# Windowed attention with global tokens and a Mish MLP on one core: the global product one unit later, a reserve on planned DMA landings, new planner constants

## The chip, the core and the metric

The kernel runs on one core of one Trainium2 chip. The metric is device time in microseconds of one execution; the time before is the median of three runs. The core has a matrix engine (PE), a vector engine (DVE), an activation engine (ACT), GpSimd (POOL), and SyncE (SP), which here issues every DMA.

## The reference

Attention with 8 batches and 8 heads of width 64: 512 local tokens see 32 global tokens and the local ones within 32 places; the 32 global tokens see all 544. The joined output, 4608 rows of 512, goes through an MLP of width 2048 whose activation is x tanh(softplus(x)) (Mish).

```python
    k_all = np.concatenate([k_g, k_l], axis=2)
    v_all = np.concatenate([v_g, v_l], axis=2)
    s_g = scale * np.matmul(q_g, k_all.transpose(0, 1, 3, 2))
    out_g = np.matmul(sm(s_g), v_all)
    s_ll = scale * np.matmul(q_l, k_l.transpose(0, 1, 3, 2))
    mask = np.abs(pos[:, None] - pos[None, :]) <= window
    s_ll = np.where(mask, s_ll, -1000000000.0)
    s_lg = scale * np.matmul(q_l, k_g.transpose(0, 1, 3, 2))
    a_l = sm(np.concatenate([s_lg, s_ll], axis=-1))
    out_l = np.matmul(a_l, np.concatenate([v_g, v_l], axis=2))
...
    h = x @ w_in
    sp = np.where(h > 20.0, h, np.log1p(np.exp(np.minimum(h, 20.0))))
    g = h * np.tanh(sp)
    return (g @ w_out).astype(np.float32)
```

The weights arrive as 64-bit floats, the rest as 32-bit. The kernel gets its accuracy on PE from pairs of f16 numbers (a high part and the rest), so that each product of the MLP and each P V takes three f16 matmuls.

## The kernel before, in words

**Attention.** The work is cut into units (batch b, head pair hp, quarter t of the 512 queries), 16 a batch and 128 in all. A unit has scores (L649 where q and k are used in f32, for the first eight pairs; L656 from f16 pairs afterwards), a masked row maximum on DVE (L662, into P), exp on ACT (L671), the split of P into high and low f16 (ph: L326 or L328, and L723), its transpose (batch 0 on PE, L695 and L700; later by a DMA transpose from ph to pt, L482), and P V (U, L740). After the fourth quarter x = U / sum is formed (L750), split (L759) and transposed into xh and xl, the input of the MLP. The global queries are done once per head pair: scores g (L780) and maximum (L794) at t = 2, exp (L802), the split of P on DVE (L814), one DMA transpose into gpt (L482), and their P V, g_pv (gu, L829: 15 matmuls), whose result ACT or DVE puts into xg. xg is the input of the MLP's last block.

**MLP.** 17 blocks of 256 rows, each in 8 steps. A step multiplies by one slice of w_in (h, L872, 24 matmuls of 256 columns), takes Mish on ACT (e, L915), splits the result into G (L328, L928 on DVE) and multiplies by one slice of w_out (o, L940, 12 matmuls of 512 columns). Twelve steps' G fit into its ring.

**Weights.** 32 pieces of 512 KB are loaded; three DVE instructions each turn 64-bit numbers into f32 (L405, L407, L414); PE sums squares (ws, L427) for a scale; then 16 splits into high and low f16 (high on ACT or DVE; low on DVE, L459). The first eight L459 are w_in's slices, the last eight w_out's. Step i of a block needs split i for h and split 8 + i for o.

**What sets the order.** The function slot(u) records the tasks of one slot in turn: the scores of unit u + 1, P V of unit u - 1, and the MLP steps that M1S puts there (h in its slot, G one later, o two later). Each task has a priority by its place in the record, the weights' tasks by a slot number of their own (CONV for conversions, FIRST for splits). Then Plan.order goes through the tasks once: it keeps a time for each engine, for the DMA queue and for every result, always takes the task that could start first (by priority where several could), and writes the tasks out in that order. So the order on every engine is fixed when the program is built. A DMA's result counts as there at its end in the queue plus DMA_OUT = 400 ns. A weight load may be issued only while the planned DMA backlog is under BULK.

Of the kernel before, what the change touches and what calls it, by code (L numbers as in the profile page):

```python
# [51 lines left out]
class Plan:  # L52
# [6 lines left out]
    DMA_IN, DMA_OUT, DMA_DEPTH = 1500, 400, 5500  # L59
    TICK, COLUMNS = 10240 / 3, 3060  # L60
    LOYAL = 800
    TABLE = 1283

    def __init__(self):
# [74 lines left out]
    def order(self):  # L139
# [9 lines left out]
        start, done, on = [None] * N, [0] * N, [None] * N  # L149
        columns = {}  # L150
        served = 0

        def tensor(t, ns, rows):

            while ns > 1e-6:
                k = int(t / self.TICK + 1e-9)
                slow = 1 if columns.get(k - 1, 0) >= self.COLUMNS else 2
                d = min(ns * slow, (k + 1) * self.TICK - t)
                columns[k] = columns.get(k, 0) + d / slow * 2.4 * rows
                ns -= d / slow  # L160
                t += d
            return t

        def enter(n):
            engs, fn, deps, after, new, pri, rows, table = self.tasks[n]
            for e, ns in engs:
                t = max([done[d] + self.HOP[on[d]][e] for d in deps] + [start[a] for a in after] + [0])
                bisect.insort(queue[e], (pri, n, ns, t))

        def first(e):  # L170

            best = None
            for pri, n, ns, t in queue[e]:
                t = max(t, free[e]) + (self.TABLE if e == ACT and self.tasks[n][7] not in (None, self.table) else 0)
                if e == DMA and len(ns) > 2:
                    t = max(t, served - ns[2])
                e0 = self.tasks[n][0][0][0]
                if e0 != e and free[e0] <= t + self.LOYAL:
                    continue
# [9 lines left out]
        for _ in range(N):  # L189
            t, pri, e, n, ns = min(c for c in map(first, free) if c)  # L190
            start[n], on[n] = t, e
            if e == ACT:
                self.table = self.tasks[n][7] or self.table
            for x, _ in self.tasks[n][0]:
                queue[x] = [c for c in queue[x] if c[1] != n]
            if e == PE:
                ns = tensor(t, ns, self.tasks[n][6]) - t
            if e == DMA:
                issue, ns = ns[:2]
                free[e] = t + issue + max(0, served - t - self.DMA_DEPTH)  # L200
                served = max(served, t + self.DMA_IN) + ns
                done[n] = served + self.DMA_OUT
            else:
                free[e] = done[n] = t + ns
            for u in users[n]:
                left[u] -= 1
                if not left[u]:
                    enter(u)
# [15 lines left out]
def attn_mish_kernel(ctx: ExitStack, tc: tile.TileContext, qt, kt, qt0, kt0, mxs, vm, vg, qg, w1, w2, consts_in, out, w64):  # L224
# [77 lines left out]
    def dma(kib):  # L302
        return 410, kib * 3.05

    def bulk(kib):
        return dma(kib) + (BULK,)

# [658 lines left out]
        UNITS[:16] = sorted(UNITS[:16], key=lambda x: (x[2] // 2, x[1], x[2]))  # L966
    steps = [(blk, i) for blk in range(NBLK) for i in range(NF)]

    LEAD0 = 13.709
    PACE = 0.958  # L970
    TAIL = 14
    M1S = []
    for s in range(len(steps)):
        at = int(LEAD0 + PACE * s) if s < 2 * NF else s + TAIL
        if s % NF == 0 and steps[s][0] < 2 * B:
# [8 lines left out]
    def att(fn, b, *a):  # L984
        pl.late = LATE_B * (b == 1)
        fn(b, *a)
        pl.late = 0

    def slot(u):
# [3 lines left out]
        fu, bu, vu = unit(u + 1), unit(u), unit(u - 1)  # L993
        b, hp, t = (u // 16, u % 16 // 4, u % 4) if bu else (0, 0, -1)
# [22 lines left out]
        if more2 and t == 3:  # L1017
            pl.late = LATE_K * (b == 0)
            k_hi(*n2)
            k_lo(*n2, 0)  # L1020
        if more1 and t == 0:
            pl.late = LATE_K * (b == 0)
            k_lo(*n1, 1)
        if more1 and t == 1:
            pl.late = LATE_K * (b == 0)
            q_hi(*n1)
# [34 lines left out]
            blk_out(m2[0])  # L1061
        if m2:
            m2_mm(*m2, 0)
        if t == 3:
            att(g_pv, b, hp)
        if m2:
            m2_mm(*m2, 1)
        if more2 and t == 1:
            pl.late = LATE_L * (b == 0)
            k_load(*n2)  # L1070
        if more2 and t == 3:
            pl.late = LATE_L * (b == 0)
            q_load(*n2)
# [11 lines left out]
        if bu and b == 0 and hp == 3 and t == 3:  # L1085
            pl.late = LATE_V
            b_load(b + 1)
# [24 lines left out]
                g_split(b + 1)  # L1112


    BULK = 2744.748
    LAG = 8
    ORDER = "k0 q0 m b k1 q1 w0 w1 g w2 w3 k2 q2 w4 w5 w6 w7 k3 q3 w8 w9 w10 w11 w12 w13 w14 w15"
    CONV1 = 10
    RATE1 = 0.05
    CONV2 = 15.31  # L1120
    RATE2 = 1.5
    FIRST1 = 9.206
    STEP1 = 1.5
    FIRST2 = 4.746
    STEP2 = 2.5
    AHEAD_DMA = 2.301
    LATE_K = 39.044
    LATE_L = 289.135
    LATE_B = 0
    LATE_V = 0  # L1130

    def weights():
        for k in range(32):
            at = CONV1 + RATE1 * k if k < 16 else CONV2 + RATE2 * (k - 16)
            if k >= 16:
                pl.slot = at - AHEAD_DMA
                w_load(k)
# [10 lines left out]
            if k == 19:  # L1148
                for j in range(8):
                    pl.slot = FIRST1 + STEP1 * j  # L1150
                    w_split(j)
        for j in range(8):
            pl.slot = FIRST2 + STEP2 * j
            w_split(8 + j)
# [4 lines left out]
    for x in ORDER.split():  # L1159
        a, n = x[0], int(x[1:] or 0)  # L1160
# [92 lines left out]
```

## Time and profile before

| | |
|---|---|
| three runs | 1061.85, 965.97, 967.1 us |
| median | 967.1 us |
| profiled execution, its own time | 966.51 us |
| its span, first to last instruction | 964.7 us |
| mean granted PE clock | 0.977 |
| PE busy, first 100 us / 100 to 200 / 200 to 800 / 800 to 900 / last 65 | 76.9 / 96.7 / 586.6 / 100.0 / 54.4 us |
| DVE busy, first 100 us / 100 to 200 / 200 to 300 | 83.6 / 87.8 / 91.7 us |
| half-clock stretches of PE in the records | 49.8 to 63.5, 70.3 to 84.0, 94.2 to 101.0, 138.6 to 142.0, and from 957.8 us |

A row of the groups gives the line, engine, operation and tiles, the shape, the count, the busy time and the mean of one in ns, then the idle time ahead of such instructions and what ended it. A row of the waits gives who waited for whom, the total in us, how often, and the longest. A row of a stage gives its borders and length, the busy time and count of PE, PE's weight loads, DVE, ACT and POOL, the granted PE clock, the share of the DMA engines and GB/s. A row in order of time gives the start, the length, the instruction, and in brackets the idle time ahead of it. Matmuls that follow each other overlap in these rows, so the time from one start to the next is what a matmul costs.

### The profile page before, as it was taken

What the parts mean: (1) busy time and instruction counts of PE and PEld (TensorE: products, weight loads), DVE (VectorE), ACT (ScalarE), POOL (GpSimd) and SP (SyncE); (2) the same over time, 40 slices, a digit from 0 to 9 for tenths busy, and PEclk for the clock granted to TensorE, in tenths of its full rate; (3) what the DMA queues carried; (4) which work ended last, traced back from release to release, by engine and by line L of the source; (5) the groups of instructions that cost most, each with busy time, mean ns of one, the idle gap of its engine ahead of it and who ended that gap; (6) DMA issues with size and microseconds to landing.
All of it is one profiled execution on the core that took longest, in us unless ns stands there. A gap on an engine that the chain in (4) does not pass through costs nothing.

```text
span 964.7 us, 20600 instructions
## 1 busy us (share of the span) xinstructions
PE 914.6 (95%) x7988; PEld 630.5 (65%) x7988; DVE 680.7 (71%) x1789; ACT 623.4 (65%) x1270; POOL 15.8 (2%) x28
## 2 busy tenths in 40 slices
PE   6787989999999999999999999999999999999995
PEld 3554774667676767667666676666666677666663
DVE  6799989788997889767777677768777755222221
ACT  4657667587876778776777777778877787211110
POOL 2000000000000000000000000000000000000000
PEclk9967999999999999999999999999999999999998
DMA  8897539988998669765576675665756342100000
GB/s 271 259 290 219 150 109 204 206 180 235 245 275 211 153 151 201 145 149 120 142 161 147 128 169 136 139 143 122 184 129 144 75 102 51 34 1 22 1 22 22
DMA packets 214010, 141.00 MB, mean 146 GB/s; under 512 B 176664, under 2 KB 188184, under 8 KB 212888
## 3 DMA queue, kind: packets, MB, share of 16 engines
q1 hardware_dynamic: 213912, 139.69, 60.2%
q8 instruction: 62, 1.02, 0.5%
q14 instruction: 36, 0.29, 0.1%
HBM read 75.15 MB, written 8.91 MB: 87 GB/s over the span
## 4 chain that ended last, share of the span: by engine, by line
PE 52%; DVE 23%; DMA 13%; ACT 4%; issue 4%; SPq 1%; DVEq 0%; ACTq 0%
PE o L940 23%; PE h L872 19%; DMA gpt<-gph 5%; DMA pt<-ph 3%; DMA vraw<-in_vm 3%; PE U L740 3%; DVE P L662 2%; PE s L656 2%; DMA kn_m<-in_mxs 2%; DVE kl L594 2%; PE s L649 2%; DVE G L928 2%; PE gu L829 2%; DVE gmx L794 1%; DVE W L407 1%
## 5 line engine op out<-in xcount | busy, mean ns | idle before, releaser
L940 PE MATMUL o<-W,G 128*128 128x512 f16 x1632 | 388.7, 379 | 0.2 <-ACT ob L326 0.2
L872 PE MATMUL h<-xh,W 128*128 128x256 f16 x2048 | 377.6, 274 | 2.3 <-ACT e L915 2.3
L872 PEld LDWEIGHTS <-W 128*128 128x128 f16 x3264 | 312.0, 98 | 66.6 <-issue 9.3
L872 PE MATMUL h<-xl,W 128*128 128x256 f16 x1024 | 280.2, 274 | 0.0
L940 PEld LDWEIGHTS <-G 128*128 128x128 f16 x1632 | 157.4, 98 | 148.0 <-issue 3.5
L915 ACT ACTIVATE e<-h,c 128x512 f32<-128x512 f32 (+1 forms) x137 | 92.7, 684 | 140.3 <-PE h L872 139.3
L671 ACT ACTIVATE P<-P,nm 128x192 f32<-128x192 f32 (+1 forms) x256 | 117.7, 460 | 52.2 <-DVE nm L662 49.9
L328 DVE TENSOR_SCALAR G<-e,c 128x512 f16<-128x512 f32 (+1 forms) x126 | 60.4, 480 | 128.7 <-ACT e L915 128.6
L662 DVE CUSTOM_DVE_ANT_0 P<-s,consts 128x192 f32<-128x192 f32 (+1 forms) x256 | 90.5, 366 | 44.1 <-PE s L656 38.3
L928 DVE SCALAR_TENSOR_TENSOR G<-e,c,G 128x512 f16<-128x512 f32 (+1 forms) x137 | 101.9, 744 | 3.0
L723 DVE SCALAR_TENSOR_TENSOR ph<-P,ph 128x384 f16<-128x384 f32 (+1 forms) x112 | 65.1, 584 | 40.0 <-ACT ph L326 39.3
L915 ACT ACT_TABLE_LOAD x62 | 79.5, 1283 | 1.1
L740 PEld LDWEIGHTS <-pt 96*128 96x128 f16 (+1 forms) x1536 | 62.7, 99 | 17.3 <-DMA pt<-ph 7.4
L671 ACT ACT_TABLE_LOAD x54 | 69.3, 1283 | 1.0
L326 ACT ACTIVATE ph<-P 128x384 f16<-128x384 f32 (+1 forms) x107 | 57.9, 545 | 11.3 <-DMA pt<-ph 9.0
L740 PE MATMUL U<-va,pt 128*128 128x64 f16 (+1 forms) x768 | 57.4, 195 | 4.9 <-DMA pt<-ph 3.9
L740 PE MATMUL U<-vc,pt 96*128 96x64 f16 x768 | 56.4, 195 | 0.0
L671 ACT ACTIVATION_READ_ACCUMULATOR P<-P,nm 128x1 f32 x256 | 47.9, 187 | 0.0
L656 PEld LDWEIGHTS <-qs 128*128 128x128 f16 x384 | 34.7, 98 | 17.9 <-issue 0.2
L649 PE MATMUL s<-kn,qn 64*128 64x192 f32 (+1 forms) x128 | 36.8, 483 | 7.3 <-DMA qn<-in_qt 4.5
L656 PE MATMUL s<-ks,qs 128*128 128x192 f16 (+1 forms) x192 | 42.2, 253 | 0.0
L656 PE MATMUL s<-kl,qs 128*128 128x192 f16 (+1 forms) x192 | 42.2, 252 | 0.0
(121 smaller groups left out, 914.2 us busy)
## 6 DMA issues: line engine op xcount, KB each, us to landing
kraw<-in_kt SPq DMA_DIRECT2D x24, 640.0 KB, 4.8
kn_m<-in_mxs SPq DMA_DIRECT2D x24, 544.0 KB, 4.9
qraw<-in_qt SPq DMA_DIRECT2D x24, 512.0 KB, 3.9
out<-ob SPq DMA_DIRECT2D x34, 256.0 KB, 2.5
vraw<-in_vm SPq DMA_DIRECT2D x8, 1024.0 KB, 6.2
wraw<-in_w SPq DMA_DIRECT2D x16, 512.0 KB, 5.3
W<-in_w SPq DMA_DIRECT2D x16, 512.0 KB, 6.2
vc<-vf SPq DMA_DIRECT2D x32, 128.0 KB, 2.4
```

What stands on the lines that cost most here:

```text
L326: A.activation(out=dst, in_=src, func=AF.Copy, scale=c)
L328: V.tensor_scalar(dst, src, c, None, ALU.mult)
L649: pl.add(PE, mm(1, 4 * w), lambda: T.matmul(X[s][:, :w], X[q][r, part, t * 128:(t + 1) * 128], X[k][r, part, c0:c0 + w], start=True, stop= ...
L656: T.matmul(X[s][:, :w], X[qs][:, h, t * 128:(t + 1) * 128], X[k][:, h, c0:c0 + w], start=(i == 0), stop=(i == 1))
L662: pl.add(DVE, 69 + 1.04 * w, lambda: V.tensor_tensor_reduce(out=X[P][:, h, :w], in0=X[s][:, :w], in1=mask[:, m0:m0 + w], scale=-SCALE, sca ...
L671: pl.add(ACT, 94 + 0.832 * w + 186, lambda: A.activation(out=X[P][:, h, :w], in_=X[P][:, h, :w], func=AF.Exp, bias=X[nm], scale=-1.0, accu ...
L723: pl.add(DVE, dve(n), lambda: V.scalar_tensor_tensor(p_part(X[ph], t, 1), p_src(X[P], t), PSC, p_part(X[ph], t, 0), ALU.mult, ALU.subtract ...
L740: T.matmul(X[u][:, t, h, :], X[pt][:k, p * 4 + h * 2 + c, :], X[vx][:k, t, vl, h * 64:(h + 1) * 64], start=(n == 0), stop=(n == 5))
L872: T.matmul(X[h][:, f * TB:(f + 1) * TB], wh(i, wl)[:, off:off + 128], X[x][:, d, o:o + TB], start=(n == 0), stop=(n == 11))
L915: chain(blk, i, ACT, 587, lambda a, z: A.activation(out=X[e][:, a:z], in_=hv(blk, i)[:, a:z], func=AF.Mish, bias=0.0, scale=X[c][:, 0:1]), ...
L928: chain(blk, i, DVE, 663, lambda a, z: V.scalar_tensor_tensor(gp(1, blk, i)[:, a:z], X[e][:, a:z], X["c", blk][:, 2:3], gp(0, blk, i)[:, a ...
L940: T.matmul(X[o], gp(g, blk, i)[:, f, t * 128:(t + 1) * 128], wh(8 + i, wl)[:, f * 512:(f + 1) * 512], start=(i == 0 and n == 0), stop=(i = ...
```

## The change

Three things change. First, g_pv of a head pair was recorded in the slot of its last quarter (t == 3); it is now recorded in the slot behind that (when the unit whose P V is taken is the last quarter). Second, the planner adds SPARE = 900 ns to a DMA's landing where the planned time is over 180 us; nothing in the program waits for it, it only puts the users of the data later in the order. Third, sixteen planner constants have new values.

```diff
+    SPARE = 900
...
-                done[n] = served + self.DMA_OUT
+                done[n] = served + self.DMA_OUT + (self.SPARE if t > 180000 else 0)
...
-    LEAD0 = 13.709
-    PACE = 0.958
-    TAIL = 14
+    LEAD0 = 20.957
+    PACE = 0.709
+    TAIL = 15
...
-        if t == 3:
-            att(g_pv, b, hp)
+        if vu and vu[2] == 3:
+            att(g_pv, *vu[:2])
...
-    BULK = 2744.748
+    BULK = 4939.749
...
-    CONV2 = 15.31
-    RATE2 = 1.5
+    CONV2 = 2.779
+    RATE2 = 1.422
```

With LEAD0, PACE and TAIL the rule for M1S gave each MLP step the slot of its number plus 17; it now gives its number plus 20. CONV1, RATE1, FIRST1, STEP1, FIRST2, STEP2, AHEAD_DMA, LATE_K, LATE_L and LATE_V are the rest of the constants. Line numbers of the changed kernel are one higher from the place where SPARE stands.

The order changes on every engine. Two places of it follow. The first is ACT in batch 4, head pair 1, from the second half of the global queries' exp (gP) to the scaling of their product (xg from gu, which PE computes just ahead). P and ph are the next pair's local units, e is Mish. Before:

```order
L802 ACTIVATE gP_1_6394,gs_1_6395<-g_1_1_6312,gmx_1_6330 64x256
L671 ACTIVATE P_74,sums_2_6398<-P_74,nm_2_0_1_6428 128x192
L326 ACTIVATE ph_80<-P_74 128x4x96
L915 ACT_TABLE_LOAD
L915 ACTIVATE e_6465<-h_6377,c_4539 128x512
L319 CAST xs_1_6486<-x_1_6482 128x512
L326 ACTIVATE xg<-gu_1_6496,sv_5322 64x32 x2
```

and now, from the row behind that gP on:

```order
L672 ACTIVATE P_74,sums_2_6252<-P_74,nm_2_0_0_6248 128x192
L916 ACT_TABLE_LOAD
L916 ACTIVATE e_2_6288<-h_2_6147,c_4789 128x512
L916 ACTIVATE e_3_6304<-h_3_6231,c_4789 128x512
L672 ACT_TABLE_LOAD
L672 ACTIVATE P_74,sums_2_6252<-P_74,nm_2_0_1_6290 128x192
L327 ACTIVATE ph_80<-P_74 128x4x96
L672 ACTIVATE P_75,sums_2_6252<-P_75,nm_2_1_0_6347 128x224
L672 ACTIVATE P_75,sums_2_6252<-P_75,nm_2_1_1_6366 128x224
L327 ACTIVATE ph_81<-P_75 128x2x224
L320 CAST xs_1_6381<-x_1_6370 128x512
L327 ACTIVATE xg<-gu_1_6399,sv_5181 64x32 x2
```

One more Mish and a whole unit of the next pair (P_75, ph_81) now stand between the global exp and the product, and Mish there belongs to a step three or four numbers lower.

The second place is DVE at the last two splits of w_out (the fifteenth and sixteenth L459; kn_m are the maxima of a later batch, vf and x belong to batch 1). Before:

```order
L814 SCALAR_TENSOR_TENSOR gph_88<-gP_1_1968,gs_1_1969,gph_88 64x544
L459 SCALAR_TENSOR_TENSOR W<-W,sw 128x1024
L723 SCALAR_TENSOR_TENSOR ph_80<-P_74,ph_80 128x4x96
L585 SCALAR_TENSOR_TENSOR qs_1_1937<-qraw_1_1824,sk_1723,qs_1_1937 64x1024
L459 SCALAR_TENSOR_TENSOR W<-W,sw 128x1024
L750 TENSOR_TENSOR x_1_2090<-U_1_1920,rs_1_1963 128x512
```

and now, from the row behind the fifteenth split on:

```order
L724 SCALAR_TENSOR_TENSOR ph_80<-P_74,ph_80 128x4x96
L528 TENSOR_REDUCE mx_3_2105<-kn_m_0_1895 128x1
L751 TENSOR_TENSOR x_1_2127<-U_1_1924,rs_1_1918 128x512
L663 ISA P_76,nm_2_2_0_2137<-s_2_2_0_2109,consts 128x224
L663 ISA nm_2_2_0_2137 128x1
L610 SCALAR_TENSOR_TENSOR vf_3_2129<-vraw_803,sv_1537,vf_3_2129 128x4x128
L760 TENSOR_TENSOR xs_1_2139<-x_1_2127,xs_1_2139 128x512
L663 ISA P_76,nm_2_2_1_2155<-s_2_2_1_2124,consts 128x224
L663 ISA nm_2_2_1_2155 128x1
L663 ISA P_74,nm_2_3_0_2158<-s_2_3_0_2142,consts 128x192
L663 ISA nm_2_3_0_2158 128x1
L460 SCALAR_TENSOR_TENSOR W<-W,sw 128x1024
```

Rows of batch 1's attention that stood behind the last split (x, its split xs, three row maxima, a v split) now stand ahead of it.

More of the change, by code (lines that the diff above doesn't have):

```diff
@@ L1112, in slot @@
                 g_split(b + 1)
-    BULK = 2744.748
+    BULK = 4939.749
     LAG = 8
     ORDER = "k0 q0 m b k1 q1 w0 w1 g w2 w3 k2 q2 w4 w5 w6 w7 k3 q3 w8 w9 w10 w11 w12 w13 w14 w15"
-    CONV1 = 10
-    RATE1 = 0.05
-    CONV2 = 15.31
-    RATE2 = 1.5
[L1122 to L1128, printed above, removed]
+    CONV1 = -2
+    RATE1 = 1.119
+    CONV2 = 2.779
+    RATE2 = 1.422
+    FIRST1 = 8.288
+    STEP1 = 1.452
+    FIRST2 = 16.719
+    STEP2 = 0.743
+    AHEAD_DMA = 4.88
+    LATE_K = 220.655
+    LATE_L = 1.986
     LATE_B = 0
-    LATE_V = 0
+    LATE_V = 106.565
     def weights():
```

## The prediction

> **What bounds the kernel now.** I read the page's first block, then the table of stages, then the waits by stage, then the order of time at the places where a wait ends.
>
> ```profile
> span 964.7 us, 20600 instructions
> PE 914.6 (95%) x7988; PEld 630.5 (65%) x7988; DVE 680.7 (71%) x1789; ACT 623.4 (65%) x1270; POOL 15.8 (2%) x28
> ```
>
> PE is busy for 95% of the span. The other 50 us, and the time at a lower clock, are what a new order can win or lose: the change adds and removes no matmul. The table of stages says where they lie (span of the stage, busy time by engine, then the granted clock):
>
> ```profile
> 0.00:20.00 20.00, 14.53 (x44) 8.29 (x44) 11.10 (x46) 10.49 (x30) 6.79 (x13) 1.00 0.82 283
> 20.00:168.00 148.00, 127.15 (x1055) 86.29 (x1054) 135.30 (x338) 96.83 (x210) 1.46 (x4) 0.87 0.73 206
> 168.00:226.00 58.00, 57.91 (x521) 38.10 (x520) 47.62 (x137) 41.31 (x99) 0.35 (x1) 1.00 0.87 188
> ```
>
> From 20 to 168 us DVE is busy for 135.3 of 148 us and PE for 127.2, at a mean clock of 0.87: here DVE, which converts the weights, sets the pace. What ends that stage is the last split of w_out, the sixteenth row of L459. In order of time, DVE's ninth and sixteenth splits and the first out-projection matmuls, then the batch-1 step of the same kind where G is what PE needs:
>
> ```profile
> 138.81 1.28 DVE L459 SCALAR_TENSOR_TENSOR W<-W,sw 128x1024 f16<-128x1024 f32 x1
> 141.84 1.55 PE L940 MATMUL o<-W,G 128*128 128x512 f16 x6
> 166.63 1.28 DVE L459 SCALAR_TENSOR_TENSOR W<-W,sw 128x1024 f16<-128x1024 f32 x1
> 167.28 4.05 PE L940 MATMUL o<-W,G 128*128 128x512 f16 x18
> 224.38 0.74 DVE L928 SCALAR_TENSOR_TENSOR G<-e,c,G 128x512 f16<-128x512 f32 x1
> 225.24 1.46 PE L940 MATMUL o<-W,G 128*128 128x512 f16 x6
> ```
>
> The ninth split ends at 140.1 and o starts at 141.8. The sixteenth ends at 167.9; the row of 18 begins with six matmuls of the step before, so the last step of block 0 starts at about 168.6. At 225 us a G ends at 225.1 and its matmul starts at 225.2. PE follows DVE to there without a gap, then DVE falls out of the path. After 168 us PE is short of work only in single waits, which the waits of PE in 180 to 850 us list (total, times, longest):
>
> ```profile
> PE gu L829 <- DMA gpt<-gph: 8.6, 9, 1.6
> PE U L740 <- DMA pt<-ph: 3.3, 5, 1.4
> PE g L780 <- DVE nm L662: 0.6, 1, 0.6
> PE o L940 <- ACT ob L326: 0.2, 1, 0.2
> ```
>
> So 12.7 us in the middle, of which 8.6 are the global queries' product waiting for its transposed probabilities. The end is the same rows in both orders and counts for nothing.
>
> **The waits in the middle.** The prices of PE work come from the chain of waits at full clock:
>
> ```profile
> 183.23 1.29 PE o L940 x6
> 184.52 0.35 PE U L740 x12
> 184.88 1.31 PE h L872 x12
> 189.15 0.44 PE gu L829 x15
> 189.59 0.63 PE s L649 x4
> ```
>
> (The last row is two score matmuls: each f32 one has two records.) In PE's order I count what stands between the last score matmul of the global queries (second g) and their product gu. For batch 4, pair 1 it was 48 h, 30 o, 24 U and 4 s, which is 5.2 + 6.5 + 0.7 + 0.3 = 12.7 us; now it is 60 h, 30 o, 24 U and 8 s, 14.5 us. Counted so over batches 3 to 7 the distance was 8 to 15 us, and is now 14 to 16, nearly everywhere the same 14.6. The largest wait was 1.6 us, so 2 to 5 us more work in between covers it. I take 8.0 of the 8.6, and as bounds 0 (something behind it is late instead) and 8.6; a loss is excluded as long as the distance grew. Of what moves with the 15 matmuls, the two scalings to xg are read only by the last block; vf and va are held a slot longer, and behind them on SP stand the seven moves of the pair after next, which in the new SP order have one transpose of P more ahead of them.
>
> The reserve of 0.9 us, together with the MLP's slots (each step three slots later than before, 20 instead of 17 after its number), puts the local products later behind their scores: the least distance from a pair's second score matmul to U, counted the same way over batches 3 to 7, goes from 9.0 to 10.8 us. Of the 3.3 us of U waits, five of at most 1.4 us, I take 2.0 away; bounds 0 and 3.3. What is late next there would be G for o: the least distance from h to its o was 4.6 us and is 8.2 in the blocks 2 and 3, and 6 to 10 in both after that, so I expect no new wait.
>
> **The DVE-bound stage.** The other constants (conversions, splits, loads, BULK, batch 1's v) only reorder what DVE, PE and SP do to 225 us, and are costed together. I count the rows of DVE ahead of the sixteenth split, before and now. The kinds are the same but for: 5 more L662, 2 more L594, one more each of L527, L609, L750, L759, of the copy to ks, and of an xg scaling (none ran on DVE before; ACT's took 0.27), and one G copy less. Prices from the groups of instructions with shapes kept apart (the last row in order of time):
>
> ```profile
> L662 DVE CUSTOM_DVE_ANT_0 P<-s,consts 128x224 f32<-128x224 f32 x128 | 46.8, 384 | 14.8 <-PE s L656 12.0 <-PE s L649 2.4
> L594 DVE SCALAR_TENSOR_TENSOR kl<-kraw,sk,ks 128x640 f16<-128x640 f32 x48 | 41.6, 866 | 0.0
> L527 DVE TENSOR_REDUCE mx<-kn_m 128x1 f32<-128x1088 f32 x24 | 30.6, 1277 | 3.5 <-DMA kn_m<-in_mxs 3.5
> L609 DVE SCALAR_TENSOR_TENSOR vf<-vraw,sv,vf 128x512 f16<-128x512 f32 x32 | 23.7, 746 | 3.5 <-ACT vf L326 3.3
> L750 DVE TENSOR_TENSOR x<-U,rs 128x512 f32<-128x512 f32 x32 | 21.9, 684 | 8.6 <-PE U L740 8.5
> L759 DVE TENSOR_TENSOR xs<-x,xs 128x512 f16<-128x512 f32 x28 | 19.2, 687 | 5.0 <-ACT xs L319 4.9
> L328 DVE TENSOR_SCALAR ks<-kraw,sk 128x1280 f16<-128x1280 f32 x14 | 12.3, 878 | 0.5 <-DMA kraw<-in_kt 0.3
> L328 DVE TENSOR_SCALAR G<-e,c 128x512 f16<-128x512 f32 x124 | 59.7, 482 | 125.9 <-ACT e L915 125.8
> 33.84 0.27 ACT L326 ACTIVATE xg<-gu,sv 64x32 f32<-64x32 f32 x1
> ```
>
> 1.9 + 1.7 + 1.3 + 0.7 + 0.7 + 0.7 + 0.9 + 0.3 less 0.5 is 7.7 us. Neighbouring rows overlap: all DVE durations of the trace add up to 780 us where the page has 680.7 busy, 0.87 of them, so the split comes 6.7 us later. Against that, PE has more of its work behind it by then. Ahead of the last step of block 0 stand 12 h, 12 U, 15 gu, 7 f32 s and 3 f32 g more: 1.3 + 0.35 + 0.45 + 2.2 + about 1.0 (g at the price of three s) is 5.3 us that needn't be done later. The end moves by 6.7 - 5.3 = +1.4 us. Bounds: +6.7 if PE gains nothing by its advance, and -9 if three quarters of DVE's 12.7 us of idle time between 20 and 168 us went. I see no reason for the latter: the largest gap of that idle is x waiting for PE's first U,
>
> ```profile
> 32.87 0.69 DVE L750 TENSOR_TENSOR x<-U,rs 128x512 f32<-128x512 f32 x1 [3.51 <-PE U L740]
> ```
>
> and in the new order the statistics of eight weight pieces instead of four (32 ws matmuls, not 16, each behind a DVE conversion) stand ahead of that U on PE, so DVE gets there later but finds it late again. At the 225 us point the new order has five more us of PE work ahead and under three more of DVE: no bound any more. Nor should a load be late, though DVE now reaches the first pieces of w_out 3 to 12 us sooner. DVE's waits on weight loads between 20 and 168 us were
>
> ```profile
> DVE W L405 <- DMA W<-in_w: 0.8, 2, 0.6
> ```
>
> and of the bytes that stand ahead of each piece in SP's new order, as many had been moved in this trace at least 1.9 us before DVE would reach the piece.
>
> The new order has one hole: between the eleventh and the twelfth split stand 25 DVE rows (7 before) of about 11 us, while PE has 7 us of work between the steps that need them. Released by the tenth split, PE would stand ready about 2 us before the twelfth. The trace shows what such a wait draws:
>
> ```profile
> 137.64 0.27 PE L872 MATMUL h<-xh,W 128*128 128x256 f16 x1 [2.19 <-ACT e L915]
> 135.20:138.60 3.40, 1.21 (x12) 0.95 (x10) 2.23 (x11) 3.36 (x6) 0.37 (x1) 1.00 0.64 141
> 138.60:142.00 3.40, 3.40 (x18) 2.44 (x17) 3.16 (x12) 2.47 (x4) 0.00 (x0) 0.50 0.37 80
> ```
>
> A wait of 2.19 us, then 3.4 us at a granted clock of 0.50: 1.7 us of matmul time lost. The splits that follow hide about half of it, so I add 0.9 us (bounds 0 and two such windows, 3.4).
> The Trainium skill (TensorE: Matmul & The Clock Gate, HAM oscillation) asks only that PE have no idle gaps over about 3.4 us. By that rule the 2 us wait would cost no clock and this term would be nothing, 957.9 in all; the trace does not agree, since 2.19 us were enough at 135 us.
>
> **What changes nothing.** LATE_K and LATE_L are used only in batch 0, for pairs whose scores take the unsplit path, so no instruction is placed by them. TAIL has no effect, since each step is put at least one slot behind the step ahead of it.
>
> **The sum.** The profiled execution took 966.5 us (span 964.7), 0.6 under the median of 967.1. 966.5 - 8.0 (gu) - 2.0 (U) + 1.4 (DVE stage) + 0.9 (clock) = 958.8 us.
>
> **Rivals.**
> *No gain (chance 0.14).* The waits are filled, but another wait takes their place: PE's order is static, and DVE and ACT follow PE in the middle, so G for o or the next score's bank (three for s, g and gu) can be late in turn. For: one gu wait stood where the distance was already 14 us. Against: DVE and ACT have a quarter of their time free there. 966.5 + 1.4 + 0.9 is about 968 us.
> *Slower (0.13).* The hole before the twelfth split and the steps behind it make PE wait at each split, and each wait draws a half-clock window; PE at half clock then loses its 5.3 us of advance. Place: 140 to 180 us. Price: 6.7 + 4 windows of 1.7 = 13.5; 966.5 - 10.0 + 13.5 = 970 us. It decides if the waits at the splits come to over 2 us each, at four of them.
> *A faster start (0.13).* The conversions that now stand earlier fill DVE's idle time. For: 12.7 us are there to fill. Against: DVE's own count went up by 6.7, and the first U is as late. With 9.5 of it gone, 958.8 - 9.5 is about 949 us.
>
> **Chances and range.** The forecast has 0.60. The range of 950 to 968 takes in the forecast, the case without gain and the slower half of the faster start; the slower case and the other half (0.20) are left out. Two per cent of the median, about what a measurement of this kernel can tell from no change, is 19.3 us: 947.8 and 986.4. Half of the faster start lies below (0.07), the far end of the slower case above (0.03), the rest (0.90) between.
>
> **What would show it.** Right: PE's gu wait under 1 us in 180 to 850 us, U under 2; the sixteenth L459 ending at 173 to 177 us, with o right behind it; a PE gap of about 2 us near 155 us with a half-clock window behind it; PE's last matmul 7 to 8 us earlier. Wrong: a gu wait still above 4 us (the distance was not the cause); the sixteenth split before 168 us (DVE's idle time went); several windows at half clock between 140 and 180 us; or new PE waits on G or nm in the middle that add up to 8 us.

## The result and the profile after

| | before | after |
|---|---|---|
| median | 967.1 us (six runs, 963.86 to 1061.85) | 958.58 us (six runs, 957.19 to 960.59) |
| ratio | | 0.9917, 95% interval 0.9896 to 0.9938 |
| profiled execution, its own time and span | 966.51, 964.7 us | 957.52, 955.7 us |
| PE's last matmul ends | 954.4 us | 945.8 us |

One execution of before (1061.85 us) and one of e6 below (2360.64 us) took far longer than the rest, and the ratios leave them out. The forecast was 958.8 us and a change within 2%; both came. Whether the reasons came too is the question of the rest. The first block of the page, after:

```profile
span 955.7 us, 20644 instructions
PE 908.4 (95%) x7988; PEld 628.1 (66%) x7988; DVE 668.0 (70%) x1774; ACT 630.5 (66%) x1283; POOL 19.6 (2%) x28
```

The matmuls are as many as before. The stages of the prediction, and the middle in two pieces (columns as before: borders, length, busy time and count of PE, PEld, DVE, ACT, POOL, granted PE clock, DMA share, GB/s), of after:

```profile
20.00:168.00 148.00, 122.56 (x1046) 84.69 (x1046) 135.58 (x348) 97.48 (x216) 2.92 (x4) 0.92 0.71 201
168.00:226.00 58.00, 55.71 (x496) 34.91 (x495) 44.40 (x130) 41.98 (x106) 0.78 (x1) 1.00 0.79 176
180.00:300.00 120.00, 114.84 (x1103) 79.11 (x1101) 101.68 (x285) 94.79 (x201) 3.93 (x4) 1.00 0.89 208
300.00:850.00 550.00, 548.82 (x5066) 386.74 (x5063) 384.93 (x1031) 402.64 (x790) 5.91 (x7) 1.00 0.63 138
```

and the last two of before:

```profile
180.00:300.00 120.00, 118.47 (x1115) 82.62 (x1116) 106.99 (x277) 92.63 (x187) 3.40 (x5) 1.00 0.96 225
300.00:850.00 550.00, 538.06 (x4992) 378.00 (x4990) 391.77 (x1055) 397.78 (x793) 4.12 (x6) 1.00 0.60 133
```

From 300 to 850 us PE is busy for 548.8 of 550 us where it was busy for 538.1: there the change wins over 10 us. From 180 to 300 us it is busy for 3.6 us less than before: there it loses some back. The waits of PE in 180 to 850 us, after:

```profile
PE U L741 <- DMA pt<-ph: 3.7, 8, 0.7
PE gu L830 <- DMA gpt<-gph: 1.7, 2, 1.0
PE h L873 <- ACT e L916: 0.7, 1, 0.7
```

gu fell from 8.6 to 1.7 us, U did not fall. The start, in DVE's and PE's order of time (the w_out splits from the twelfth split on; PE's steps that need them, and its two waits for o; then x, which waited for PE's first U):

```profile
154.03 1.27 DVE L460 SCALAR_TENSOR_TENSOR W<-W,sw 128x1024 f16<-128x1024 f32 x1
...
172.47 1.28 DVE L460 SCALAR_TENSOR_TENSOR W<-W,sw 128x1024 f16<-128x1024 f32 x1
```

```profile
136.70 0.38 PE L941 MATMUL o<-W,G 128*128 128x512 f16 x1 [0.69 <-ACT W L327]
138.02 0.81 PE L941 MATMUL o<-W,G 128*128 128x512 f16 x3 [0.94 <-DVE W L460]
...
156.22 1.47 PE L941 MATMUL o<-W,G 128*128 128x512 f16 x6
...
175.59 1.69 PE L941 MATMUL o<-W,G 128*128 128x512 f16 x7
```

```profile
38.85 0.69 DVE L751 TENSOR_TENSOR x<-U,rs 128x512 f32<-128x512 f32 x1 [4.09 <-PE U L741]
```

The sixteenth split ends at 173.75 us (forecast 173 to 177; before 167.9), and the last step of block 0 starts at 175.6 (before 168.6).

**A ledger of PE's time.** To compare orders that do the same work in another sequence, I take for a matmul its start less the priced PE work ahead of it (prices as in the prediction: h 0.109, o 0.216 us, and so on; 887.3 us in all). It grows where PE waits or runs at half clock. One price is too high (g's), so it sinks by 7 to 8 us from 300 to 850 us in a kernel that never waits; differences between kernels hold. From one matmul's start to the next, less the price, it also says what each wait really cost.

| us | before | after | difference | of it gu | U | all else |
|---|---|---|---|---|---|---|
| at the last step of block 0 | 57.0 | 58.5 | +1.5 | | | |
| growth from there to 300 us | +2.2 | +6.0 | +3.8 | +2.0 | +1.9 | -0.1 |
| growth from 300 to 850 us | +7.7 | -6.0 | -13.7 | -11.6 | -1.7 | -0.4 |

The sum is -8.4 us; PE's last matmul came 8.6 us sooner.

### The profile page after: what moved, and what is told of

Read it like the earlier page. It is cut to its first block, busy times and chain, and to the rows that moved or that the text cites. A ratio compares the mean times of both kernels' runs of the same rounds, so it can differ in the third digit from the quotient of the medians.

```text
span 955.7 us, 20644 instructions
## 1 busy us (share of the span) xinstructions
PE 908.4 (95%) x7988; PEld 628.1 (66%) x7988; DVE 668.0 (70%) x1774; ACT 630.5 (66%) x1283; POOL 19.6 (2%) x28
## 4 chain that ended last, share of the span: by engine, by line
PE 67%; DVE 18%; DMA 8%; ACT 3%; issue 2%; SPq 1%; POOL 0%; DVEq 0%; ACTq 0%
PE o L941 29%; PE h L873 27%; PE U L741 3%; DMA pt<-ph 3%; PE s L657 3%; DMA kn_m<-in_mxs 2%; PE g L781 2%; DVE W L415 2%; DVE W L408 2%; DVE P L663 2%; DMA vraw<-in_vm 1%; PE s L650 1%; DVE W L460 1%; DMA gpt<-gph 1%; DVE mx L528 1%
## 5 line engine op out<-in xcount | busy, mean ns | idle before, releaser
L327 ACT ACTIVATE ph<-P 128x384 f16<-128x384 f32 (+1 forms) x112 | 61.0, 546 | 14.5 <-DMA pt<-ph 12.3
L803 ACT ACTIVATE gP<-g,gmx 64x288 f32<-64x288 f32 x64 | 30.3, 474 | 21.7 <-DVE gmx L798 21.6
```

The source lines that it names most:

```text
L327: A.activation(out=dst, in_=src, func=AF.Copy, scale=c)
L803: pl.add(ACT, 464, lambda part=part, c0=c0, c1=c1: A.activation(out=X[P][:, c0:c1], in_=X["g", b, hp, part][:64, 0:c1 - c0], func=AF.Exp, ...
```

## The experiments

Two theories stood at the outset. *Distance* (the prediction's): gu waited because too little PE work stood between the global scores and their product; g_pv one unit later is what ends it. *Plan*: the waits come from where the planner put loads, transposes and engines' work around g_pv, and the reserve (or the new constants) is what ends them, with or without the distance. All ratios are to the kernel before on the chip of that run, where its median was 966.3 to 967.1 us.

| kernel | median us | ratio, interval | start (last step of block 0) | growth to 300 | waits of gu, U, others from 300 to 850, start to start |
|---|---|---|---|---|---|
| before | 967.1 | 1 | 57.0 | 2.2 | 11.6, 3.0, 0.6 |
| after | 958.58 | 0.9917 [0.9896, 0.9938] | 58.5 | 6.0 | 0, 1.3, 0.7 |
| e1 after, g_pv back | 960.72 | 0.9941 [0.9918, 0.9963] | 58.5 | 6.8 | 3.4, 0, 0.2 |
| e2 after, no reserve | 973.21 | 1.0070 [1.0047, 1.0093] | 59.8 | 18.2 | 0, 2.6, 4.5 |
| e3 before, g_pv later | 965.67 | 0.9986 [0.9968, 1.0004] | 56.0 | 3.8 | 0, 6.7, 4.2 |
| e4 before, reserve | 959.33 | 0.9928 [0.9907, 0.9949] | 56.4 | 1.6 | 1.9, 5.5, 1.9 |
| f1 before, reserve on gpt | 961.93 | 0.9966 [0.9939, 0.9992] | 56.3 | 4.6 | 1.6, 6.1, 0.6 |
| f1b before, reserve on all but gpt | 960.08 | 0.9936 [0.9913, 0.9960] | 56.6 | 6.9 | 3.6, 2.2, 1.1 |
| f3 after, reserve in 180 to 260 us | 964.12 | 0.9982 [0.9968, 0.9996] | 57.1 | 8.5 | 0, 0.8, 3.9 |
| e8 before, new weight constants | 983.39 | 1.0176 [1.0147, 1.0205] | 70.9 | 2.1 | 11.5, 7.2, 1.7 |
| h1 before, key load held | 962.85 | 0.9960 [0.9946, 0.9974] | 55.1 | 3.1 | 3.5, 2.2, 6.6 |
| x1 after, reserve 2700 | 956.98 | 0.9897 [0.9877, 0.9916] | 59.0 | 4.4 | 0, 1.6, 0 |
| e5 after, old weight constants | 973.91 | 1.0076 [1.0056, 1.0097] | 61.9 | 18.8 | 0, 0, 0.9 |
| e6 after, old slots of the MLP | 963.91 | 0.9967 [0.9951, 0.9983] | 67.2 | 2.2 | 0, 0, 4.6 |

(The last three columns come from one profiled execution each, in us.) The six profiles whose order up to 180 us is that of before have a start of 55.1 to 57.0, the five with that of after 57.1 to 59.8: one profile's start is good to about 1 us. The growth to 300 us hangs on g's price as well and is no better than that; e5's is what makes the ledger end where PE's last matmul does. Some profiled executions are not typical of their kernel: those of e2, e4 and f1b took 2.6 to 2.9 us more than the median, those of e3 and f3 2.9 and 2.4 us less.

### e1: g_pv back in its old place

```diff
-        if vu and vu[2] == 3:
+        if vu and vu[2] == 3 and vu[0] < 3:
             att(g_pv, *vu[:2])
+        if t == 3 and b >= 3:
+            att(g_pv, b, hp)
```

> The changed kernel with the global product back at its old place from batch 3 on; the order up to batch 2 is that of the changed kernel. Theory (the distance from the global scores to gu ends the gu waits, and a wait of PE in the middle is paid one for one): the distance falls from 14 to 16 us to 8.3 to 14.2, PE's gu waits come back from 1.7 to 7 to 9 us, and the time rises by 5 to 7 us to 964 to 966. Rival (the lag of the MLP by three more slots has made room everywhere, so that the place of gu no longer matters): gu waits stay under 3 us and the time within 1.5 us of 958.6.

With the work between g and gu back to 8 to 14 us from batch 3 on, PE's waits were

```profile
PE gu L830 <- DMA gpt<-gph: 3.1, 7, 0.8
PE U L741 <- DMA pt<-ph: 3.0, 6, 1.1
PE gu L830 <- DVE ph L724: 1.1, 1, 1.1
PE h L873 <- ACT e L916: 0.7, 1, 0.7
```

and the median 2.1 us above after. With the old distance (11.5 us in the mean of batches 3 to 7, before 11.2) gu's waits are 4.2 us in the list, against 1.7 in after and 8.6 in before. The time rose by less than half of what I had expected. The distance from g is part of the cause at most.

### e2: the change without the reserve

```diff
-    SPARE = 900
+    SPARE = 0
```

> The changed kernel without the reserve on planned landings (0 instead of 900 ns). The order up to 180 us of planned time is that of the changed kernel. Theory as in the prediction (the reserve takes 2 us of U waits away): U waits rise from 3.7 to 5 to 7 us, the time by about 2 us to 960.5. Rival (the reserve has no use, since U waits were 3.3 us before it and are 3.7 with it): U waits 3 to 4.5, time within 1 us of 958.6.

Slower than before, and 14.6 us above after. Most of it lies in one place. Two stages of 3.4 us, PE's two long waits, and the place as a whole with what lies around it, in e2:

```profile
233.70:237.10 3.40, 1.56 (x18) 0.82 (x17) 3.40 (x11) 2.37 (x9) 0.05 (x1) 1.00 1.17 310
237.10:240.50 3.40, 0.00 (x0) 0.00 (x0) 3.16 (x15) 2.01 (x4) 0.32 (x1) 0.51 1.06 243
```

```profile
240.72 0.34 PE L741 MATMUL U<-va,pt 128*128 128x64 f16 x3 [4.01 <-DMA pt<-ph]
245.10 0.37 PE L873 MATMUL h<-xh,W 128*128 128x256 f16 x1 [3.56 <-ACT e L916]
```

```profile
219.00:237.00 18.00, 14.93 (x175) 10.70 (x171) 16.58 (x44) 10.83 (x34) 0.00 (x0) 1.00 0.92 211
237.00:251.00 14.00, 6.72 (x35) 4.04 (x36) 13.20 (x37) 6.89 (x13) 0.37 (x1) 0.51 0.99 221
251.00:265.00 14.00, 14.00 (x129) 9.83 (x128) 8.01 (x17) 4.58 (x9) 0.37 (x1) 1.00 0.83 265
```

U waited 4.0 us for its transposed probabilities, the MLP then 3.6 us for Mish, and PE stood at a clock of 0.51 for 13.65 us. In e2's order U of batch 2 stands as little as 4.2 us of PE work behind its scores; in after's, where the planner counts each landing 0.9 us later, 12.9 us. Up to 300 us the ledger grows by 12.2 us more than in after, nearly all of it at this place, and from 300 us on by 5.2 more (these two profiled executions lie 18.6 us apart, the medians 14.6).

### e3 and e4: each edit alone on the kernel before

e3 has g_pv one unit later from batch 3 on, and nothing else; e4 has the reserve, and nothing else.

```diff
-        if t == 3:
+        if t == 3 and b < 3:
             att(g_pv, b, hp)
+        if vu and vu[2] == 3 and vu[0] >= 3:
+            att(g_pv, *vu[:2])
```

> The kernel before with only the global product one unit later, from batch 3 on; the order up to batch 2 is that of the kernel before. Theory: gu waits fall from 8.6 to 1 to 2 us, the time from 967.1 to about 960 (959 to 962). Rival (lag and constants made the gain): gu waits fall, but others (U, G) take their place, and the time stays at 965 to 968.

> The kernel before with only the reserve of 900 ns. Theory as in the prediction: U waits 3.3 to about 1.3 us, gu waits lower by up to 3 us too, since the reserve counts for the landing of gpt as well; time 962 to 965. Rival (no use): both waits within 1 us of before, time 966 to 968.

PE's waits in 180 to 850 us in e3, then in e4:

```profile
PE U L740 <- DMA pt<-ph: 6.7, 6, 2.3
PE s L656 <- ACT gP L802: 2.6, 5, 0.9
PE gu L829 <- DMA gpt<-gph: 1.1, 2, 0.6
PE s L656 <- DVE nm L662: 0.9, 2, 0.5
```

```profile
PE U L741 <- DMA pt<-ph: 5.0, 3, 2.3
PE gu L830 <- DMA gpt<-gph: 2.0, 3, 1.1
PE h L873 <- ACT e L916: 1.1, 2, 0.6
PE s L657 <- ACT gP L803: 0.7, 1, 0.7
```

In e3 gu's waits went as the distance theory wants, and U and s took their place: 0.9 us of gain in the median, with an interval that takes in no gain at all. That is the prediction's "no gain" rival, in a kernel with g_pv alone. In e4 gu's waits went too, though g_pv was not touched, and the time with them: -7.3 us by the medians, nearly the whole gain of the change. The profiled execution of e4 is its slowest (962.25 us): two of its waits each drew a half-clock window, at 328 and 495 us. So moving g_pv is not needed. But e4 alone does not say that the distance plays no part: the planner, which now counts gpt later, left the distance from g as it was in the mean (11.4 us, before 11.2), yet stretched it from 9.8 to 12.8 us in the pairs (4, 0), (5, 0) and (6, 0) (batch, head pair), which in before had 4.5 of the 11.6 us of waits. The next runs take the two apart.

### f1, f1b, f3: on which landings the reserve works, and when

```diff
+                done[n] = served + self.DMA_OUT + (self.SPARE if t > 180000 and ns == 250 + 160 * 4.7 else 0)
```

That is f1, with the reserve on gpt's transposes alone; f1b has `!=`, every DMA but those. f3 is the changed kernel with the reserve only where 180000 < t < 260000.

> The kernel before with the reserve of 900 ns on the landing of the global transposes (gpt) alone. Theory (before's loss in the middle is gpt landing later than planned, and the reserve on it gives the gain of the run with the reserve alone): gu waits fall from 8.6 to 2 to 3 us, U waits stay near 3, time 960 to 962. Rival (the gain came from the transposes of P and the other DMAs, or from the new order as such): time 965 to 968.

> The kernel before with the reserve on every DMA but the global transposes. Theory: gu waits stay at 7 to 9 us, time 964 to 967. Rival (the reserve works through the transposes of P and the loads): time 959 to 962 though the gu waits stay.

> The changed kernel with the reserve only for DMAs planned between 180 and 260 us. Theory (without the reserve the changed order puts a local product 4 us behind its scores in batch 2, PE waits 4 us for it and 3.6 for the Mish behind it, and 14 us pass at half clock; that one place is the reserve's whole worth there): no half-clock window between 105 and 940 us, time 958 to 962. Rival (the reserve earns its 15 us all along the middle): time 966 to 972.

In f1b the planner does not know of any later gpt, and PE's work between g and gu is 8.3 us at least, as before (11.0 in the mean, 11.2 before). Still gu's waits fell to

```profile
PE gu L830 <- DMA gpt<-gph: 2.1, 5, 0.6
```

so the reserve does not need to place gu later behind its transpose: in the pairs (4, 0), (5, 0) and (6, 0) PE reaches gu 2.7 to 2.9 us after the transpose's issue (before 3.0), and the transposes landed in 3.1 to 3.7 us (before 4.2 to 4.7). What it changed is the traffic around gpt, next. In f1 it does place gu later: in the same pairs PE reaches gu 4.7 us after the issue, and no wait is left though two of the three landings are as late as in before. f3 has no such place as e2's at 240 us, but its theory (no half-clock window) failed: U waited 2.0 us at 284 us and one window at half clock followed. f3 is 9.1 us faster than e2 and 5.5 slower than after. So of the 14.6 us that the reserve is worth in the new order, some 9 belong to the DMAs planned between 180 and 260 us, where the place in batch 2 lies, and some 5 to the rest.

### h1: the key load taken out of gpt's way

In SP's records of before I looked for what stands ahead of gpt. The transposes of batches 3 to 7 with a bulk load issued less than 2.2 us ahead of them landed 4.2 to 5.7 us after their issue (mean 4.7, six with a record), the others after 2.8 to 3.9 (mean 3.1, nine). So h1 is the kernel before with one rule more: from 300 us on the planner takes the 640 KB load of the next raw keys 2.5 us later than it could.

```diff
+                if e == DMA and t > 300000 and len(ns) == 2 and ns[1] == 640 * 3.05:
+                    t += self.HOLD
```

> The kernel before with one rule more in its planner: from 300 us on, the 640 KB load of the next raw keys (kraw) is taken 2.5 us later than it could be. Nothing else is touched: g_pv stands where it stood (8.3 us of TensorE's work behind its scores at least, median 11.2, before 8.3 and 11.6), U too (9.6 at least, before 9.0), no reserve, the same constants. In the planned order of the DMA queue the key load then stands directly ahead of none of the 20 transposes of gpt of batches 3 to 7; before it stands directly ahead of 10 of them. In the trace of before the transposes with a key load issued 0.7 to 2.0 us ahead were followed by gu 4.1 to 5.8 us after their issue, those without by 2.9 to 4.5. Theory 'the landing': TensorE's waits for gpt come from that load in the way, so they fall from 8.6 us to 3 or less though the distance is the same; the time is 966.5 less 5 to 6, with some of it lost where the splits of the later keys are awaited: 961.5 (959 to 964). Rival 'the distance', on which the prediction rested: the distance is unchanged, so the waits stay at 7 to 9 us and the time at 966.5. Second rival: the key loads land later and TensorE waits for scores instead: 968 or more.

The pair (3, 3), SP and then PE, in before (kraw is the load, gpt the transpose; the bracket is PE's wait):

```profile
403.70 0.35 SPq L315 DMA_DIRECT2D kraw<-in_kt  x1
404.39 1.43 SPq L482 DMA_TRANSPOSE gpt<-gph  x1
```

```profile
410.15 0.25 PE L829 MATMUL gu<-gpt,va 128*128 128x64 f16 x3 [1.51 <-DMA gpt<-gph]
```

and in h1:

```profile
404.34 1.33 SPq L485 DMA_TRANSPOSE gpt<-gph  x1
405.83 1.23 SPq L485 DMA_TRANSPOSE pt<-ph  x1
407.16 0.53 SPq L318 DMA_DIRECT2D qgraw<-in_qg  x1
407.74 0.43 SPq L318 DMA_DIRECT2D kraw<-in_kt  x1
```

```profile
407.36 0.25 PE L832 MATMUL gu<-gpt,va 128*128 128x64 f16 x3
```

The transpose is issued at the same time to 0.05 us. With the key load 0.7 us ahead of it gu starts 5.8 us after that issue, with the load behind it 3.0 us after and without a listed wait, though the distance from g is 1.3 us less there. Over the kernel:

```profile
PE U L743 <- DMA pt<-ph: 3.9, 6, 0.9
PE s L659 <- ACT gP L805: 2.8, 3, 1.3
PE gu L832 <- DMA gpt<-gph: 2.6, 3, 1.1
PE h L875 <- ACT e L918: 2.0, 3, 0.9
```

gu's waits fell from 8.6 to 2.6 us (start to start from 11.6 to 3.5), as the landing theory expected (3 or less), with no more distance from g than before in the mean (10.7 us, before 11.2). Pair by pair the new order did move it: at (5, 0) and (6, 0) it is 2.9 us longer and the transpose is issued 1.5 us later, so part of what these two gained is room and not landing. At (4, 0), where no key load is near any more, the landing still took 4.1 us and gu waited 1.1 us, so the load is not the only thing that delays a landing. The time fell by 4 us and not by 5 to 6, because 2.8 us of waits of s and 2.0 of h came up. So gu waited in before for a chain with three terms: PE's distance, set against the time from g to the transpose's issue (4 to 13 us) plus the landing (2.8 to 5.7 us). Pair (5, 0) of before is the model: 9.8 us of distance against 7.0 + 4.5.

The first two terms make one: the room, which is the time from the transpose's issue to gu, less gu's wait. The means over batches 3 to 7 (of the landings that have a record) tell the runs apart:

| kernel | g to gu, PE's work | room | landing | gu's waits |
|---|---|---|---|---|
| before | 11.2 | 3.4 | 3.7 | 11.6 |
| e1 | 11.5 | 4.7 | 3.8 | 3.4 |
| f1 | 12.2 | 4.4 | 3.6 | 1.6 |
| f1b | 11.0 | 3.5 | 3.2 | 3.6 |
| h1 | 10.7 | 3.8 | 3.1 | 3.5 |
| e4 | 11.4 | 4.4 | 3.2 | 1.9 |
| after | 14.5 | 6.7 | 3.5 | 0 |

f1 adds room at before's landing, f1b shortens the landing at before's room, and either takes away most of the waits; e4 has both. e1 has before's distance and landing, but its transposes are issued sooner behind g (7.1 us, before 8.2), which is room too.

### e8, e5, e6: which of the new constants need each other

e8 is the kernel before with only the new weight constants (BULK, CONV, RATE, FIRST, STEP, AHEAD_DMA, LATE). e5 is the changed kernel with those as before. e6 is the changed kernel with

```diff
-    LEAD0 = 20.957
-    PACE = 0.709
-    TAIL = 15
+    LEAD0 = 13.709
+    PACE = 0.958
+    TAIL = 14
```

> The kernel before with only the new constants for conversions, splits, loads and batch 1's v (BULK, CONV, RATE, FIRST, STEP, AHEAD_DMA, LATE_V), the MLP's slots as before. Theory (until 170 us the end is set by the worst of: DVE's work ahead of a w_out split, less PE's work ahead of the matmul that needs it): here that difference is 47.1 us by the rows' prices, at the ninth to eleventh split, against 37.4 before and 39.2 in the changed kernel, so the first out-projection step starts with 8 to 10 us more lost, and the time is 974 to 978. Rival (the new weight constants are what makes the start better): time 960 to 966.

> The changed kernel with the constants of the weights' loading and splitting as before (BULK, CONV, RATE, FIRST, STEP, AHEAD_DMA and LATE): g_pv one unit later, the reserve, and the second stage's start at unit 20 stay. By VectorE's count of work less TensorE's ahead of the splits the start is 37.9, before 37.4, after 39.2: by that the last step of the first output comes 1.3 us less late than after. U stands at least 10.0 us behind its scores from batch 3 on, but only 5.5 in batch 2, where after has 12.9 and the kernel without the reserve, which lost 9 us between 219 and 251 us, had 4.2. Theory 'the place in batch 2 is set by distance': TensorE waits there 2 to 4 us and draws half-clock windows, for 4 to 9 us: 963 to 967, say 965. Rival 'the reserve heals it': no such wait, 957.5 (956 to 960).

> The changed kernel with the second stage's start as before (LEAD0 13.709, PACE 0.958, TAIL 14 in place of 20.957, 0.709, 15); g_pv, the reserve and the new constants of the weights stay. VectorE's count of work less TensorE's ahead of the splits has its maximum at 45.2, before 37.4 and after 39.2. Theory 'the count sets the start': after the last split the ledger of time less TensorE's work stands 57.0 + 45.2 - 37.4 = 64.8, which is 6.3 above what after has there (58.5); with the rest as after, 958.5 + 6.3 = 965 (963 to 968), more if the wait draws a half-clock window. Rival 'the count is no measure here': the new constants load the weights early enough for either lag and the time is 958.5 (957 to 961).

The expectations of all three count DVE's work ahead of each w_out split less PE's ahead of the step that needs it; the largest of the eight differences should set the start. For e8 the count said 9.7 us more than before, 57.0 + 9.7 = 66.7 in the ledger; the first o stood at 66.8. But the step behind the last split stood at 70.9, and the median came out 5 us above the upper end of what I gave: the size failed, not the direction. In e8 gu's waits are what they are in before (11.5 us), so the weight constants do nothing for them.

For e6 the count said 64.8; the ledger has 67.2 there, and the median is 963.9 of an expected 965. Ahead of the first o two waits for Mish drew two half-clock windows, of at most 1.7 us each; whether these make the 2.4 us above the count stays open:

```profile
119.50:122.90 3.40, 0.86 (x8) 0.77 (x8) 3.40 (x6) 3.04 (x5) 0.00 (x0) 1.00 0.48 70
122.90:126.30 3.40, 3.40 (x21) 2.53 (x20) 2.66 (x5) 0.00 (x0) 0.00 (x0) 0.51 0.40 149
133.20:136.60 3.40, 0.50 (x5) 0.45 (x5) 3.23 (x5) 3.37 (x5) 1.27 (x1) 1.00 0.35 77
136.60:140.00 3.40, 3.40 (x14) 1.82 (x13) 3.07 (x12) 3.32 (x5) 0.06 (x1) 0.50 0.55 121
```

e5 was expected at 965 by the distance in batch 2 (5.5 us from scores to U, in spite of the reserve) and came out at 973.9. The mechanism stood: the ledger grows by some 19 us up to 300 us, most of it between 220 and 250 us, as in e2. The size did not: I had priced that place at 4 to 9 us. PE waited there for U, s and h in turn, 7 us in all, and two stretches at half clock of 13.65 and 3.4 us came with it. At the start PE had its work done early and waited 11.3 us for a split of w_out that the old constants bring later:

```profile
152.34 0.58 PE L941 MATMUL o<-W,G 128*128 128x512 f16 x1 [11.34 <-ACT W L327]
```

The wait itself cost nothing, the ledger is 54.9 there; the 13.65 us at half clock that followed took it to 59.1 within one step.

So slots, weight constants and reserve belong together: against before, the weight constants alone give +17 us, the change without them +7, the change without the later slots -3, without the reserve +7, and all of it -8.5. The later slots alone were not run.

### x1: a larger reserve

```diff
-    SPARE = 900
+    SPARE = 2700
```

> The changed kernel with the reserve three times as large (2700 in place of 900). Counted in TensorE's priced work, U then stands at least 11.5 us behind its scores from batch 3 on (after: 10.8) and 15.9 in batch 2 (after: 12.9), gu 13.9 to 18.0 (after: 13.9 to 15.9); the start is the same to the instruction. Theory 'waits': what is left of TensorE's waits between 180 and 850 us, 3.7 for pt, 1.7 for gpt and 0.7 for h, falls to some 2 in all, and the time by 3 to 4: 955 (953 to 957.5). Rival 'used up': the remaining waits are the chip's own differences from the plan and only change their places: 958.5 (957 to 961).

```profile
PE s L657 <- ACT gP L803: 1.5, 1, 1.5
PE U L741 <- DMA pt<-ph: 1.3, 2, 0.9
PE h L873 <- ACT e L916: 1.3, 1, 1.3
PE gu L830 <- DMA gpt<-gph: 0.9, 1, 0.9
```

The waits of U and gu fell from 5.4 to 2.2 us, those of s and h rose from 0.7 to 2.8 (without nm's 0.3). The median of 956.98 is 1.6 us under after's, with intervals of the ratio that overlap and spans of the profiled executions of 955.3 and 955.7: perhaps a little faster, not shown.

## Why the prediction was right, step by step

That the sum came within 0.3 us of the median is luck: three of its four terms were off, by 0.9 to 2.2 us, and their errors cancelled. The direction and the rough size were earned by the waits of PE for gpt, which were there to win and were won.

| term | predicted | measured, from the ledger |
|---|---|---|
| gu waits | -8.0 | -9.6 (-11.6 from 300 us on, +2.0 before that) |
| U waits | -2.0 | +0.2 (-1.7 and +1.9) |
| start, DVE against PE | +1.4 | +1.5 |
| half-clock window in the hole | +0.9 | 0 |
| all else | 0 | -0.5 |
| sum | -7.7 | -8.4, and -9.0 between the profiled executions |

**The gu term** was mis-sized in two ways that partly cancel. The bound "8.0 of the 8.6" took the waits' idle time as their whole price. Start to start the 15 waits from 300 us on cost 11.6 us: the list names nine. Its idle time is counted from the modelled end of the last matmul, and an h matmul has 0.27 us there but takes 0.11 from one start to the next, so each listed wait cost 0.16 us more than it shows, and six shorter ones are not listed. Against that, two new gu waits of 0.97 and 0.70 us came up in batches 1 and 2, at pairs whose distance had grown (from 11.9 to 12.8 us and from 14.5 to 20.4), which "a loss is excluded as long as the distance grew" ruled out. At the second the transpose was issued 16.8 us behind g and landed in 5.5: the distance from g says nothing where the issue moves with it.

**The cause I gave for it** was one of three. "2 to 5 us more work in between covers it" is true: in after the transposes of batches 3 to 7 are issued 3.4 to 10.4 us ahead of gu and land in 2.8 to 4.7, and from 300 us on no gu waits. But the longer distance from g is not what carries the change: e1 takes it away for 2.1 us, e3 brings it alone for 0.9 us, which the interval does not tell from nothing, e4 has 7.3 us of the gain without moving g_pv, and f1b and h1 have before's mean distance and a third of the waits. The prediction gave the reserve 2.0 us; in the new order it is worth 14.6 (e2). I read the wait's name (gpt) and asked only how far ahead g stood; I did not ask what else was on the queue when gpt was issued.

**The U term** failed as a step. "The least distance goes from 9.0 to 10.8 us" is right, and U's waits from 300 us on did fall, by 1.7 us. Up to 300 us, for which I had not counted the distance, they rose by 1.9: six delays of 3.7 us in all, before five of 1.8.

**The start** held, in size and in its markers: the sixteenth split ends at 173.75 us, 5.8 later than before (6.7 forecast), o 1.8 us behind it (0.7 before), x still waiting for U (4.09 us, before 3.51). The method is confirmed by e8's first step and, less closely, by e6. Its size is uncertain by the 1 us by which equal orders differ; between the means of the two groups of profiles it is +2.4.

**The clock term** failed. PE did stand ready in the hole, but not for 2 us: the step behind the twelfth split (ends 155.30) began at 156.22 without a wait. What waits there were came as 0.69 and 0.94 us at 136 to 138, which put 1.56 us of idle time into one window, and as 1.31 us at 129 in another; the windows behind them stayed at full clock, and no window between 104 and 950 us was at half clock. Before had one. The Trainium skill's rule (TensorE: Matmul & The Clock Gate, HAM oscillation), which asks only for no idle gap over 3.4 us, gave nothing for this term and was right on it here; e6, f3 and e2 show that it is not a safe rule, below.

**The rivals.** "No gain" happened to e3, the change with g_pv alone. "Slower" happened, at another place and by another price than mine: not at the splits from 140 to 180 us but at U of batch 2, 220 to 250 us, in e2 and e5; with the new slots, the reserve and the new weight constants are both needed to stay clear of it. I had looked for a collapse at the one place where I counted a hole, and not at the pairs where the distance from scores to U was least; I had counted that distance for batches 3 to 7 only. "A faster start" did not come: x was as late as ever.

So the sum was right by its largest term, with 1.6 us too little gain there, and 2.2 us too much for U, 0.9 too much loss for the clock. Of the signs named for being right, the split and PE's last matmul (8.6 us sooner, 7 to 8 forecast) came or nearly so; gu's waits under 1 us (1.7), U's under 2 (3.7) and the gap with a half-clock window did not. None of the signs for being wrong came.

## What to carry to other kernels

A wait names the transfer that came last, not its cause: before moving the consumer, look at what the queue issued in the 2 us ahead of that transfer; a bulk load there went with a landing of 4.7 us in place of 3.1 here, and holding the load for 2.5 us took away two thirds of the waits. Measure the room from the transfer's issue to its consumer, and not from the first result of the chain. In this program, whose order is fixed by a planner, a margin on the planned landings was worth more than the move of one product (7.3 us against 0.9, each alone), and constants that were found together should be tried together: the weight constants alone lost 17 us. Count the least distance from a result to its user over the whole program, the part with the densest traffic above all, since one place that is too short costs its wait and then a stretch at half clock.

## What the hardware did that I had not expected

**Half clock follows a window with too little work, not only one long gap.** The half-clock stretches come in multiples of 3.41 us and start on one grid per execution. I added PE's idle time in each such window from 103 to 850 us in thirteen profiles (all but e8). Twelve windows at full clock with 1.95 to 3.41 us of idle time were followed by a window at half clock, and so were two with less, 1.58 us (e5) and 1.86 us (e2). One window with 2.03 us (h1) was not, and none of the others, which had up to 1.70 us. The gaps need not be one: in e2 the window from 233.7 us on had 1.56 us of work in several pieces, with no gap over 1.0 us, and was followed by half clock, while single gaps of 1.56 to 1.69 us were not. But the sum of idle time does not sort them all (1.58 us drew half clock, 2.03 did not). The work in the window does: counted as the columns that the matmuls started in it stream (256 for an h, 512 for an o, 64 for U or gu, times the share of the 128 rows that they use), the fourteen had 0 to 3264, and all others 3328 or more, where a window full of h has some 8000 (256 in 0.109 us). The margin is narrow, one run (f3, 3264) sets its lower end, and no run was made to test it. A stretch goes on while its windows are idle: after 11.3 us (e5) and 4.0 and 3.6 us (e2) of waits it lasted four windows. The Trainium skill (TensorE: Matmul & The Clock Gate, What's actually happening) gives a free-running window of 3413 ns, which these stretches agree with, and one idle window as what brings the low state; here a window that was busy for nearly half of its time (1.4 to 1.8 of 3.41 us) was idle enough.

**A DMA transpose lands later behind a bulk load.** Issue to landing of gpt in batches 3 to 7, with and without such a load less than 2.2 us ahead: 4.7 and 3.1 us in before, 4.3 and 2.9 in e1, 4.1 and 2.9 in after, 4.3 and 2.9 in x1, 4.3 and 3.2 in e3, and less far apart in e4, f1 and f1b (3.6 to 3.9 against 2.9 to 3.5); in h1, where no landing on record has such a load ahead of it, 3.1. In e4 two landings behind a key load issued 2.0 us ahead took 3.0 us all the same, so the load delays a landing often and not always.
